# Turning the cached keys in 32x32 blocks on VectorE in place of 128x128 transposes on TensorE, in a decode kernel

## The chip, the cores and the metric

The kernel runs on one core of a Trainium2 chip; the other seven do nothing. The metric is the device time of one execution in microseconds, median of the runs. The core has TensorE (matrix multiplication, PE in the profile; PEld is its weight load), VectorE (DVE), ScalarE (ACT), GpSimd (POOL) and SyncE (SP), whose queue issues nearly all transfers here. All data is float32. [...]

## The reference, cut to what matters

One decode step of a transformer block for 8 sequences: a modulated layer norm, attention over a window of a cache, a projection, a second modulated norm and an MLP with squared ReLU.

```python
B, D, Hq, Hkv, Sk, Dh = 8, 512, 32, 8, 8192, 128     # W = 2048, rep = 4
mod = (silu(c) @ w_mod).reshape(8, 6, 1, -1)          # sa, ca, ga, sb, cb, gb
h = layernorm(x) * (1 + ca) + sa
q = (h @ wq)                                          # 8 x 32 heads x 128
k = repeat(k_cache[:, :, Sk - W:, :], rep, axis=1)    # last 2048 rows
v = repeat(v_cache[:, :, Sk - W:, :], rep, axis=1)
p = softmax(einsum("bhqd,bhkd->bhqk", q, k) * Dh ** -0.5)
o = einsum("bhqk,bhkd->bhqd", p, v)
x = x + ga * (o @ wo)
h = layernorm(x) * (1 + cb) + sb
x = x + gb * (relu(h @ w1 + b1) ** 2 @ w2 + b2)
```

K and V of the window are 67.1 MB each (8 x 8 x 2048 x 128 floats); with the weights about 165 MB come from HBM. Each key is used by four query heads only.

## The kernel before, in words

**Loads.** `pump` issues a list of loads in a fixed order on SP's queue. A load needs a free slot: there are two "big" slots (32 KB per partition, `K_SLOTS`) and five "small" ones (16 KB, `V_SLOTS`). A load whose slot isn't free makes SP wait, and all loads behind it wait too. `("K", q)` is a block of 4.2 MB: the keys of one KV head (`hk = q // 2`) for four sequences, on partitions `4 p + u` (`u` is the sequence, `p` runs over 32 pieces of the window), 64 cache rows of 128 floats each. `("V", v)` is 2.1 MB. The order is K0, four pieces of `w_mod`, four of `wq`, K1, V0, K2, V1, K3, V2, V3, K4, and from there on two V blocks to a K block, with three pieces of `wo` between them; at the end come the last part of `wo` with half of `w1` (`tail`, a big slot), the rest of `w1` (small) and `w2` (big). `done(key)` gives a slot back after the last instruction that reads it.

**Steps.** The attention runs in 32 steps `s` (half a K block each) and some more for the V blocks, which lag by `PV_LAG = 5` steps. In each step, for two of the four parts `g` of a K block:

- `transposes(q, g, e)` (L232, L234): TensorE turns eight 128x128 pieces, so that the head dimension lies on the partitions; the result is in PSUM (`kt_ps`). Two copies of 128x512, one by ACT and one by DVE, take it to `kT` in SBUF, sorted by sequence `u`. The last one of a block calls `done(("K", q))`.
- `scores(q, g)` (L358): four matmuls of 512 columns, one for each sequence `u`, side by side in four column groups of TensorE. They add into `s_ps`, whose rows are (u, part, query head); a window cut from `qwin` (queries between zeros) selects the rows.
- `weighted(v, h)` (L450): weights times V; then four DVE instructions (L464, L466) pick the diagonal blocks out of `o_ps`.

Once for each of the eight KV heads come `soft_a` to `soft_d` (copy of the scores, maximum, exponent at L402 on ACT, DVE copy at L410, eight TensorE transposes at L426 with two DVE multiplications at L429) and later `gather` and `project_o`.

**Order.** The program is written with a manual schedule: each engine executes its instructions in the order in which the code issues them. An instruction that waits holds back all behind it on its engine.

**Before the steps.** Modulation (L294), queries (L319), and `turn_q` (L330 to L334), which puts the queries on the partitions by head dimension (`qall`); `window` copies those of one KV head into `qwin` (L344). The first K block is turned early: `EARLY` lists its parts, three of which are turned between the matmuls of the modulation and the fourth in step 0.

Of the kernel before, what the change touches and what calls it, by code (L numbers as in the profile page):

```python
# [20 lines left out]
def tile_adaln_cached_attention_mlp(  # L21
# [34 lines left out]
    ktp = ctx.enter_context(tc.tile_pool(name="ktp", bufs=3))  # L56
    ps_kt = ctx.enter_context(tc.tile_pool(name="ps_kt", bufs=2, space=bass.MemoryType.PSUM))
# [127 lines left out]
    qall = consts.tile([P, HKV, B, REP], F32, name="qall")  # L185
    qwin = [consts.tile([P, B, 60], F32, name=f"qwin{i}") for i in range(2)]
    for t in qwin:
        nc.gpsimd.memset(t, 0.0)

# [8 lines left out]
    u4 = consts.tile([P, 4], F32, name="u4")  # L198
    nc.vector.tensor_reduce(u4, ident.rearrange("p (u x) -> p u x", u=4), axis=AX.X, op=ALU.add)
    for c in range(2):  # L200
        nc.vector.tensor_scalar(bq[:, 4 * c : 4 * c + 4], u4, uq[:, c : c + 1], None, op0=ALU.mult)
# [11 lines left out]

    mine = consts.tile([P, 2, REP], F32, name="mine")
    odd = ident.rearrange("p (r u) -> p u r", u=2)
    for u in range(2):
        nc.vector.tensor_reduce(mine[:, u, 0:1], odd[:, u, :], axis=AX.X, op=ALU.add)
        for t in range(1, REP):
            nc.vector.tensor_copy(mine[:, u, t : t + 1], mine[:, u, 0:1])

    KTS = {}

    def transposes(q, g, e):

        k = slot(("K", q), DH)
        if e == 0:
            KTS[q, g] = ktp.tile([P, 4, 16, 32], F32, name="kT")
        t = KTS[q, g]
        for a in range(2):
            p = ps_kt.tile([P, 4, P], F32, name="kt_ps")  # L230
            for i in range(4):
                nc.tensor.transpose(p[:, i, :], k[:, 32 * e + 16 * a + 4 * g + i, :], ident)  # L232
            i = 8 * e + 4 * a
            (nc.vector.tensor_copy if a else nc.scalar.copy)(  # L234
                t[:, :, i : i + 4, :], p.rearrange("p i (r u) -> p u i r", u=4)
            )
        if g == 3 and e == 1:
            done(("K", q))
# [24 lines left out]
    EARLY = [(0, g) for g in range(4)]  # L263
# [64 lines left out]
    def turn_q(r):  # L328
# [3 lines left out]
        for t in range(REP):  # L332
            nc.tensor.transpose(pT_[:, t * P : (t + 1) * P], qs[:, t * P : (t + 1) * P], ident)  # L333
        nc.vector.tensor_copy(  # L334
            qall[:, 4 * r : 4 * r + 4].rearrange("p g b t -> p t g b"),
            pT_.rearrange("p (t g b) -> p t g b", t=REP, g=4)[:, :, :, :B],
        )
# [4 lines left out]
    P_, PT_, RZ_, RZP_, OS_, O_, MX_, SS_ = {}, {}, {}, {}, {}, {}, {}, {}  # L342
    def window(hk):
        nc.vector.tensor_copy(qwin[hk % 2][:, :, 28:32], qall[:, hk])  # L344

    def scores(q, g):

        hk, c = divmod(q, 2)
        if c == 0 and g == 0:
            s_ps[0] = ps_1.tile([P, 512], F32, name="s_ps")  # L350
            if hk == 0:
                window(0)
        if c == 1 and g == 0 and hk + 1 < HKV:
            window(hk + 1)
        o = 28 - 4 * (2 * g + c)
        kT = KTS.pop((q, g))
        for u in range(4):
            nc.tensor.matmul(  # L358
                s_ps[0][32 * u : 32 * u + 32, :],
                qwin[hk % 2][:, 4 * c + u, o : o + 32],  # L360
                kT[:, u].rearrange("p i r -> p (i r)"),
                start=(c == 0 and g == 0),
                stop=(c == 1 and g == 3),
            )
# [8 lines left out]
    def soft_b(hk):  # L373
        pm = ps_m.tile([P, 512], F32, name="m_ps", tag="m_ps")
# [5 lines left out]
            pm[0:1, :P].rearrange("p (u g r) -> p u r g", u=4, g=4),  # L380
# [3 lines left out]
        nc.vector.tensor_scalar(  # L384
            mrow.rearrange("p u (g r) -> p u g r", g=4),
            m1.rearrange("p (u r) -> p u r", u=4)[:, :, None, :].to_broadcast([1, 4, 4, 8]),
            -SCALE,
            None,
            op0=ALU.mult,
        )  # L390
        MX_[hk] = mrow

    def soft_c(hk):
# [6 lines left out]
        pr = work.tile([P, 8, H, 2], F32, name="pr", bufs=1)  # L400
        z = work.tile([P, 1], F32, name="z")
        nc.scalar.activation(  # L402
            pr.rearrange("p i (r e) u -> p e i r u", e=2)[:, :, :, :, 0],
            SS_.pop(hk).rearrange("p (e i r) -> p e i r", e=2, i=8),
            AF.Exp,
            bias=nm,
            scale=SCALE,
            accum_out=z,
        )
        nc.vector.tensor_copy(pr[:, :, :, 1], pr[:, :, :, 0])  # L410
        zs = work.tile([P, B], F32, name="zs")
        nc.vector.tensor_scalar(zs, bq, z, None, op0=ALU.mult)  # L412
        P_[hk], RZP_[hk] = pr, zs
# [5 lines left out]
    def soft_d(hk):  # L419

        pr = P_.pop(hk)
        PT_[hk] = work.tile([P, 2, 4 * C, 4, 2 * REP], F32, name="pT", bufs=1)
        for a in range(2):
            pp = ps_m.tile([P, 512], F32, name="m_ps", tag="m_ps")
            for i in range(4):
                nc.tensor.transpose(  # L426
                    pp[:, i * P : (i + 1) * P], pr[:, 4 * a + i].rearrange("p r u -> p (r u)"), ident
                )
            nc.vector.tensor_mul(  # L429
                PT_[hk][:, a].rearrange("p x i r -> p i x r"),  # L430
                pp.rearrange("p (i x r) -> p i x r", i=4, r=2 * REP),
# [232 lines left out]
```

## Time and profile before

| | us |
|---|---|
| median of 3 runs | 397.13 (397.06 to 397.26) |
| the profiled execution: its time | 397.39 |
| the profiled execution: span, first to last instruction | 395.6 |
| PE busy | 330.5 (84%) |
| DVE busy | 178.2 (45%) |
| ACT busy | 97.5 (25%) |
| mean granted TensorE clock | 0.974 |

The page gives busy time for each engine and, in 40 slices, the share of the 16 DMA engines that was busy. A second view, of stretches of time, gives the same for windows that one chooses. The group rows read: line, engine, operation, result <- operands, shape, count | busy us in all, mean ns of one | idle time of the engine ahead of them and what ended it. The chain of waits goes back from the last instruction to what released each step; its rows are start, length, what. Waits of SP's queue (SPq) show when a load was held back for a slot.

### The profile page before, as it was taken

To read this page: it belongs to the slowest core of one execution; us is meant where nothing else is said; L and a number is where in the kernel's file an instruction comes from. 1 tells how busy PE (TensorE), PEld (TensorE's weight loads), DVE (VectorE), ACT (ScalarE), POOL (GpSimd) and SP (SyncE) were. 2 spreads that over 40 slices of the span, in tenths; PEclk is the share of its full clock that TensorE was granted. 3 is DMA by queue.
4 is the path that set the end of the run, shared out by engine and by line. 5 is a ranking of instruction groups with operands and counts; after the bars stand their busy time and mean duration, and the time that the engine had idled before them with its cause. 6 is when DMAs were issued, how large, how long until landed. Compare 5 with 4: busy or idle time off the path is not lost.

```text
span 395.6 us, 5981 instructions
## 1 busy us (share of the span) xinstructions
PE 330.5 (84%) x2550; PEld 162.4 (41%) x2550; DVE 178.2 (45%) x416; ACT 97.5 (25%) x169; POOL 2.4 (1%) x12
## 2 busy tenths in 40 slices
PE   0683489979998697999889988998859998997696
PEld 0440035554454353444444544444534454432133
DVE  6121023454456353655464556454524455455531
ACT  2220022342232122322332222222211241222010
POOL 2000000000000000000000000000000000000000
PEclk9996889999999998999999999999999999999999
DMA  8999999999999999999999999999999999999993
GB/s 335 410 430 427 441 418 442 417 419 446 404 435 442 414 432 422 441 417 451 403 449 409 444 416 434 434 419 421 437 419 447 417 437 413 431 431 421 422 424 136
DMA packets 10363, 165.22 MB, mean 418 GB/s; under 512 B 1112, under 2 KB 1376, under 8 KB 1632
## 3 DMA queue, kind: packets, MB, share of 16 engines
q1 hardware_dynamic: 10192, 164.71, 97.9%
q8 instruction: 20, 0.33, 0.3%
q10 hardware_dynamic: 144, 0.13, 0.1%
q14 instruction: 7, 0.06, 0.0%
HBM read 164.77 MB, written 0.07 MB: 417 GB/s over the span
## 4 chain that ended last, share of the span: by engine, by line
DMA 46%; PE 42%; DVE 7%; ACT 4%; issue 1%; ACTq 0%; DVEq 0%
DMA big<-in_A_k_cache_dram 31%; PE kt_ps L232 20%; PE s_ps L358 9%; PE o_ps L450 7%; DMA small<-in_A_wq_dram 6%; DMA big<-in_B_w_dram 5%; DMA small<-in_A_v_cache_dram 4%; ACT pr L402 2%; DVE o_sb L466 2%; DVE kT L234 2%; PE m_ps L294 1%; ACT kT L234 1%; DVE pT L429 1%; PE m_ps L319 1%; DVE pr L410 1%
## 5 line engine op out<-in xcount | busy, mean ns | idle before, releaser
L232 PE MATMUL kt_ps<-ident,big 128*128 128x128 f32 x1024 | 145.5, 285 | 22.6 <-DMA big<-in_A_k_cache_dram 18.3
L232 PEld LDWEIGHTS kt_ps<-ident,big 128*128 128x128 f32 x1024 | 112.8, 144 | 111.9 <-ACT kT L234 68.1
L234 DVE COPY kT<-kt_ps 128x512 f32<-128x512 f32 x128 | 88.2, 689 | 121.5 <-PE kt_ps L232 121.5
L234 ACT COPY kT<-kt_ps 128x512 f32<-128x512 f32 x128 | 75.0, 586 | 209.4 <-PE kt_ps L232 208.6
L358 PE MATMUL s_ps<-kT,qwin 128*32 128x512 f32 x512 | 69.2, 614 | 0.8 <-DVE qwin L344 0.8
L450 PE MATMUL o_ps<-small,pT 128*32 128x512 f32 x512 | 67.1, 602 | 1.9 <-DMA small<-in_A_v_cache_dram 1.9
L466 DVE SCALAR_TENSOR_TENSOR o_sb<-o_ps,diag,o_sb 128x128 f32<-128x128 f32 x96 | 33.7, 351 | 3.4
L319 PE MATMUL m_ps<-small,h1T 128*32 128x512 f32 x64 | 11.5, 857 | 11.5 <-DMA small<-in_A_wq_dram 11.5
L450 PEld LDWEIGHTS o_ps<-small,pT 128*32 128x32 f32 x512 | 11.7, 108 | 22.7 <-issue 22.7
L464 DVE TENSOR_SCALAR o_sb<-o_ps,diag 128x128 f32<-128x128 f32 x32 | 11.2, 350 | 16.3 <-PE o_ps L450 15.6
L358 PEld LDWEIGHTS s_ps<-kT,qwin 128*32 128x32 f32 x512 | 10.3, 109 | 12.8 <-issue 11.1
L402 ACT ACTIVATE pr<-ss,nm 128x512 f32<-128x512 f32 x8 | 9.9, 1244 | 11.8 <-DVE nm L399 11.7
L334 DVE COPY qall<-m_ps 128x128 f32<-128x128 f32 x2 | 0.8, 390 | 23.0 <-PE m_ps L333 23.0
L435 PE MATMUL m_ps<-zs,tsel 128*128 128x8 f32 x16 | 3.1, 266 | 8.7 <-DVE pT L429 8.7
L319 PEld LDWEIGHTS m_ps<-small,h1T 128*32 128x32 f32 x64 | 2.1, 134 | 19.8 <-DMA small<-in_A_wq_dram 10.6
L429 DVE TENSOR_TENSOR pT<-m_ps,mine 128x512 f32<-128x512 f32 x16 | 10.2, 680 | 0.0
L474 PE MATMUL m_ps<-o_sb,pick 128*128 128x512 f32 x16 | 8.4, 606 | 1.8 <-DVE o_sb L466 1.6
L426 PEld LDWEIGHTS m_ps<-ident,pr 128*128 128x128 f32 x64 | 6.9, 141 | 7.0 <-issue 7.0
L426 PE MATMUL m_ps<-ident,pr 128*128 128x128 f32 x64 | 8.7, 278 | 1.1 <-DVE zs L412 1.1
L370 DVE TENSOR_REDUCE mx<-ss 128x1 f32<-128x512 f32 x8 | 5.5, 688 | 8.6 <-ACT ss L368 8.6
L410 DVE COPY pr<-pr 128x512 f32<-128x512 f32 x8 | 3.4, 430 | 12.3 <-ACT pr L402 12.3
L294 PE MATMUL m_ps<-small,cT 128*32 128x512 f32 (+1 forms) x64 | 6.6, 531 | 1.3 <-DMA small<-in_w_mod_dram 1.3
(123 smaller groups left out, 105.4 us busy)
## 6 DMA issues: line engine op xcount, KB each, us to landing
big<-in_A_k_cache_dram SPq DMA_DIRECT2D x16, 4096.0 KB, 21.9
small<-in_A_v_cache_dram SPq DMA_DIRECT2D x32, 2048.0 KB, 23.2
small<-in_A_wq_dram SPq DMA_DIRECT2D x4, 2048.0 KB, 21.8
small<-in_w_mod_dram SPq DMA_DIRECT2D x4, 1536.0 KB, 17.4
small<-in_A_wo_dram SPq DMA_DIRECT2D x3, 2048.0 KB, 19.9
big<-in_A_wo_dram SPq DMA_DIRECT2D x2, 1024.0 KB, 17.8
big<-in_B_w_dram SPq DMA_DIRECT2D x1, 2048.0 KB, 23.4
big<-in_B_w_dram SPq DMA_DIRECT2D x1, 1792.0 KB, 22.0
```

The lines of the kernel that those rows point to most:

```text
L232: nc.tensor.transpose(p[:, i, :], k[:, 32 * e + 16 * a + 4 * g + i, :], ident)
L234: (nc.vector.tensor_copy if a else nc.scalar.copy)(t[:, :, i : i + 4, :], p.rearrange("p i (r u) -> p u i r", u=4))
L294: nc.tensor.matmul(pm[32 * q : 32 * q + 32, : (m1 - m0) * P].rearrange("p (m n) -> p m n", n=P), cT[:, kc, :], wv[:, m0:m1, q, :], start=( ...
L319: nc.tensor.matmul(pqs[r][32 * g : 32 * g + 32, :], hT[:, kc, :], w[:, 4 * r + g, :], start=(kc == 0), stop=(kc == NQ - 1),)
L358: nc.tensor.matmul(s_ps[0][32 * u : 32 * u + 32, :], qwin[hk % 2][:, 4 * c + u, o : o + 32], kT[:, u].rearrange("p i r -> p (i r)"), start ...
L402: nc.scalar.activation(pr.rearrange("p i (r e) u -> p e i r u", e=2)[:, :, :, :, 0], SS_.pop(hk).rearrange("p (e i r) -> p e i r", e=2, i= ...
L426: nc.tensor.transpose(pp[:, i * P : (i + 1) * P], pr[:, 4 * a + i].rearrange("p r u -> p (r u)"), ident)
L429: nc.vector.tensor_mul(PT_[hk][:, a].rearrange("p x i r -> p i x r"), pp.rearrange("p (i x r) -> p i x r", i=4, r=2 * REP), mine.rearrange ...
L450: nc.tensor.matmul(o[32 * g : 32 * g + 32].rearrange("p j d -> p (j d)"), PT_[hk][:, h, 4 * c + g].rearrange("p i r -> p (i r)"), v[:, j : ...
L464: nc.vector.tensor_scalar(d, o[:, 0, :], diag[:, 0:1], None, op0=ALU.mult)
L466: nc.vector.scalar_tensor_tensor(d, o[:, j, :], diag[:, j : j + 1], d, op0=ALU.mult, op1=ALU.add)
L474: nc.tensor.matmul(pp, pick.rearrange("p t u -> p (t u)"), o.rearrange("p c d -> p (c d)"), start=True, stop=True)
```

## The change

`transposes(q, j, e)` now is one DVE instruction, a transposition of 32x32 blocks: for 32 of the block's 64 cache rows it takes 32 of the 128 head dimensions (part `j`) and turns the 32 by 32 squares of each group of 32 partitions. A square's 32 columns are partitions `4 p + u`; they are written sorted by sequence, `u * 8 + p`, so that each sequence has runs of eight. In the order in which the engine writes, `u` runs fastest, with steps of eight floats. There is no `kt_ps` any more, and no copy of it.

Since a group of 32 partitions keeps its own pieces of the window, the result has on its partitions (group `i`, 32 dimensions) in place of 128 dimensions. The queries therefore are laid out as a block matrix over `i`: `turn_q` writes `qbd` with four copies on 32 partitions (L328), and `window` makes `qst` by one matmul with `sel` and eight small copies, four on ACT and four on DVE (L346). Row order of the scores changes; a matmul with a permutation (`perm`, L378) brings it back, and the exponent reads that result in PSUM and writes contiguously. The weights are turned by DVE too (L424, 1024 elements per partition), after two multiplications by a mask, one on DVE and one on ACT (L412, L410). `kT` has two buffers, not three; `EARLY` holds parts 0 and 1 of the first K block, where it held all four.

```diff
-    EARLY = [(0, g) for g in range(4)]
+    EARLY = [(0, 0), (0, 1)]
...
-        if kc < 3:
+        if kc < 2:
             transposes(0, kc, 0)
             transposes(0, kc, 1)
...
-    def transposes(q, g, e):
+    def transposes(q, j, e):
 
         k = slot(("K", q), DH)
         if e == 0:
-            KTS[q, g] = ktp.tile([P, 4, 16, 32], F32, name="kT")
-        t = KTS[q, g]
-        for a in range(2):
-            p = ps_kt.tile([P, 4, P], F32, name="kt_ps")
-            for i in range(4):
-                nc.tensor.transpose(p[:, i, :], k[:, 32 * e + 16 * a + 4 * g + i, :], ident)
-            i = 8 * e + 4 * a
-            (nc.vector.tensor_copy if a else nc.scalar.copy)(
-                t[:, :, i : i + 4, :], p.rearrange("p i (r u) -> p u i r", u=4)
-            )
-        if g == 3 and e == 1:
+            KTS[q, j] = ktp.tile([P, 64, 4, 8], F32, name="kT")
+        rows = slice(32 * e, 32 * e + 32)
+        nc.vector.transpose(
+            KTS[q, j][:, rows].rearrange("q r u p -> q r p u"),
+            k[:, rows, 32 * j : 32 * j + 32].rearrange("q r (p u) -> q r p u", u=4),
+        )
+        if j == 3 and e == 1:
             done(("K", q))
...
-        nc.vector.tensor_copy(
-            qall[:, 4 * r : 4 * r + 4].rearrange("p g b t -> p t g b"),
-            pT_.rearrange("p (t g b) -> p t g b", t=REP, g=4)[:, :, :, :B],
-        )
+        for j in range(4):
+            b = slice(32 * j, 32 * j + 32)
+            nc.vector.tensor_copy(
+                qbd[b, 4 * r : 4 * r + 4, j].rearrange("p g (b t) -> p t g b", t=REP),
+                pT_[b].rearrange("p (t g b) -> p t g b", t=REP, g=4)[:, :, :, :B],
+            )
...
     def window(hk):
-        nc.vector.tensor_copy(qwin[hk % 2][:, :, 28:32], qall[:, hk])
+
+        pq = ps_1.tile([P, 512], F32, name="q_ps")
+        nc.tensor.matmul(pq[:, :P], sel, qbd[:, hk].rearrange("p j x -> p (j x)"), start=True, stop=True)
+        pv = pq[:, :P].rearrange("p (j c u t) -> p c u j t", j=4, c=2, u=4)
+        for i in range(4):
+            b = slice(32 * i, 32 * i + 32)
+            for c in range(2):
+                (nc.vector.tensor_copy if c else nc.scalar.copy)(
+                    qst[hk % 2][b, 4 * c : 4 * c + 4, :, i, c], pv[b, c]
+                )
...
-                s_ps[0][32 * u : 32 * u + 32, :],
-                qwin[hk % 2][:, 4 * c + u, o : o + 32],
-                kT[:, u].rearrange("p i r -> p (i r)"),
+                s_ps[0][32 * u : 32 * u + 32, :].rearrange("q (r p) -> q r p", p=8),
+                qst[hk % 2][:, 4 * c + u, j].rearrange("p i c t -> p (i c t)"),
+                kT[:, :, u],
...
-        for a in range(2):
-            pp = ps_m.tile([P, 512], F32, name="m_ps", tag="m_ps")
-            for i in range(4):
-                nc.tensor.transpose(
-                    pp[:, i * P : (i + 1) * P], pr[:, 4 * a + i].rearrange("p r u -> p (r u)"), ident
-                )
-            nc.vector.tensor_mul(
-                PT_[hk][:, a].rearrange("p x i r -> p i x r"),
...
+        nc.vector.transpose(
+            PT_[hk].rearrange("p u j r -> p j u r"),
+            X_.pop(hk).rearrange("p j (u r) e c -> p j u (r e c)", u=4),
+        )
...
-        if s == 0:
-            transposes(0, 3, 0)
-            transposes(0, 3, 1)
```

Two places show how DVE's order moves. The first lies around the first scores. `qall` and `qbd` are the queries by head dimension, `qwin` and `qst` the queries as the score matmuls read them, `big_88` is the slot of K0 in the changed kernel and `big_89` that of K1. Before:

```order
L310 TENSOR_SCALAR mul<-m_ps,lo 128x128
L334 COPY qall<-m_ps 128x4x32
L344 COPY qwin_115<-qall 128x8x4
L234 COPY kT<-kt_ps 128x4x128 x2
L334 COPY qall<-m_ps 128x4x32
L234 COPY kT<-kt_ps 128x4x128 x3
L344 COPY qwin_116<-qall 128x8x4
L234 COPY kT<-kt_ps 128x4x128 x6
```

The same place in the changed kernel:

```order
L302 TENSOR_SCALAR mul<-m_ps,lo 128x128
L328 COPY qbd<-m_ps 32x4x4x8 x4
L346 COPY qst_112<-q_ps 32x16x4 x4
L328 COPY qbd<-m_ps 32x4x4x8 x4
L225 STREAM_TRANSPOSE kT<-big_88 128x32x8x4 x4
L225 STREAM_TRANSPOSE kT<-big_89 128x32x8x4 x3
L346 COPY qst_113<-q_ps 32x16x4 x4
L225 STREAM_TRANSPOSE kT<-big_89 128x32x8x4 x5
```

Before, the last copies of K0 (two on DVE) lie between the two `qall` copies. Now half of K0 (four transpositions) comes behind all copies of the queries, eight to `qbd` and four to `qst`, and K1 follows at once.

The second place is one softmax in the middle of the attention. Before:

```order
L370 TENSOR_REDUCE mx<-ss 128x1
L234 COPY kT<-kt_ps 128x4x128
L464 TENSOR_SCALAR o_sb<-o_ps,diag 128x128
L466 SCALAR_TENSOR_TENSOR o_sb<-o_ps,diag,o_sb 128x128 x3
L234 COPY kT<-kt_ps 128x4x128
L378 TENSOR_REDUCE m_1230<-m_ps 1x32
L384 TENSOR_SCALAR mrow<-m_1230 1x128
L234 COPY kT<-kt_ps 128x4x128
L399 COPY nm<-m_ps 128x1
L410 COPY pr<-pr 128x512
L412 TENSOR_SCALAR zs<-bq,z 128x8
L234 COPY kT<-kt_ps 128x4x128 x2
```

The same place in the changed kernel:

```order
L373 TENSOR_REDUCE mx<-ss 128x1
L225 STREAM_TRANSPOSE kT<-big_88 128x32x8x4
L458 TENSOR_SCALAR o_sb<-o_ps,diag 128x128
L460 SCALAR_TENSOR_TENSOR o_sb<-o_ps,diag,o_sb 128x128 x3
L225 STREAM_TRANSPOSE kT<-big_88 128x32x8x4
L384 TENSOR_REDUCE m_688<-m_ps 1x32
L390 TENSOR_SCALAR mrow<-m_688 1x128
L225 STREAM_TRANSPOSE kT<-big_88 128x32x8x4
L399 COPY nm<-m_ps 128x1
L412 TENSOR_SCALAR pr_704<-pr,uq 128x512
L414 TENSOR_SCALAR zs<-bq,z 128x8
L225 STREAM_TRANSPOSE kT<-big_88 128x32x8x4 x2
```

Each 128x512 copy of keys from PSUM has become a transposition of 1024 elements per partition, read straight from the slot; the number of DVE instructions for the keys stays the same, and ACT's copies of the same number are gone.

More of the change, by code (lines that the diff above doesn't have):

```diff
@@ L182, in tile_adaln_cached_attention_mlp @@
     s_ps = [None]
[L185 to L187 removed]
+    qbd = consts.tile([P, HKV, 4, B * REP], F32, name="qbd")
+    qst = [consts.tile([P, B, 4, 4, 2, REP], F32, name=f"qst{i}") for i in range(2)]
+    for t in [qbd, *qst]:
         nc.gpsimd.memset(t, 0.0)
```

74 lines of the change are left out of this document (31 added, 43 removed).

## The prediction

> **What bounds the kernel now.** I read the DMA part of the page first, then stretches of time, the chain of waits and the waits of SP's queue, last the groups by line and shape. The first fence has the page's DMA queue and the stretches (start:end, length, busy us and count by engine, granted clock, DMA share, GB/s).
>
> ```profile
> q1 hardware_dynamic: 10192, 164.71, 97.9%
> ```
>
> ```profile
> core 0: us, PE busy (x) PEld busy (x) DVE busy (x) ACT busy (x) POOL busy (x), PEclk, DMA share, GB/s
> 0.00:20.00 20.00, 7.69 (x42) 5.22 (x43) 8.64 (x42) 4.80 (x8) 2.43 (x12) 1.00 0.90 370
> 20.00:40.00 20.00, 12.08 (x96) 4.80 (x98) 4.31 (x9) 2.88 (x6) 0.00 (x0) 0.83 1.02 433
> 40.00:60.00 20.00, 12.93 (x90) 4.26 (x86) 2.34 (x5) 2.25 (x4) 0.00 (x0) 0.83 1.00 429
> 192.68:231.66 38.98, 36.18 (x280) 18.27 (x281) 20.45 (x44) 11.04 (x19) 0.00 (x0) 1.00 1.01 430
> ...
> 353.99:390.73 36.74, 28.57 (x237) 10.45 (x237) 17.20 (x52) 3.84 (x8) 0.00 (x0) 1.00 0.95 399
> 390.73:395.60 4.87, 1.72 (x48) 1.19 (x48) 0.58 (x2) 0.00 (x0) 0.00 (x0) 1.00 0.09 27
> ```
>
> The transfers bound it. From 20 us on the DMA engines are busy all the time at about 428 GB/s, although PE works 36.18 of 38.98 us in the stretch of four steps. The chain (start, length, what) and SP's longest wait show how close the two are:
>
> ```profile
> 211.35 20.18 DMA big<-in_A_k_cache_dram
> 231.66 1.07 PE kt_ps L232 x8
> ...
> 353.99 15.81 DMA small<-in_A_v_cache_dram
> 369.82 20.87 DMA big<-in_B_w_dram
> 390.73 1.76 PE m_ps L617 x48
> ```
>
> ```profile
> SPq L108 <- PE kt_ps L232: 250.9, 30, 27.3
> ```
>
> SP always waits until PE has turned a K block, then the next K takes 20.18 us to land, where 4.2 MB at 428 GB/s need 9.8: some 10 us of transfers are queued ahead of it. That reserve hides PE. Freeing PE therefore buys nothing while the transfers run without a gap; what can cost is a slot that comes free too late. Four steps need 39.0 us of transfers (two K, four V), 44 with a piece of `wo`.
>
> **The part that decides: one transposition.** Removed are 1024 PE transposes, 75.0 us of copies on ACT and 88.2 us on DVE; added are 128 DVE transpositions of 1024 elements per partition. The rows that bear on their price T:
>
> ```profile
> L232 PE MATMUL kt_ps<-ident,big 128*128 128x128 f32 x1024 | 145.5, 285 | 22.6 <-DMA big<-in_A_k_cache_dram 18.3 <-ACT kT L234 3.4
> ...
> L234 DVE COPY kT<-kt_ps 128x512 f32<-128x512 f32 x128 | 88.2, 689 | 121.5 <-PE kt_ps L232 121.5
> L234 ACT COPY kT<-kt_ps 128x512 f32<-128x512 f32 x128 | 75.0, 586 | 209.4 <-PE kt_ps L232 208.6 <-DVE kT L234 0.8
> ...
> L402 ACT ACTIVATE pr<-ss,nm 128x512 f32<-128x512 f32 x8 | 9.9, 1244 | 11.8 <-DVE nm L399 11.7
> ...
> L478 DVE STREAM_TRANSPOSE tr<-m_ps 128x512 f32<-128x512 f32 x8 | 5.7, 717 | 3.3 <-PE m_ps L474 3.3
> ...
> L334 DVE COPY qall<-m_ps 128x128 f32<-128x128 f32 x2 | 0.8, 390 | 23.0 <-PE m_ps L333 23.0
> L243 DVE STREAM_TRANSPOSE rc<-m_ps 128x448 f32<-128x448 f32 x1 | 0.7, 650 | 1.3 <-PE m_ps L598 1.3
> L554 DVE COPY at_i<-wo_ps 128x256 f32<-128x256 f32 x1 | 0.4, 425 | 1.2 <-PE wo_ps L490 1.2
> ...
> L276 ACT ACTIVATE sq<-xc_in,nmean 128x128 f32<-128x128 f32 x1 | 0.4, 402 | 5.9 <-DVE nmean L273 5.9
> ...
> L555 ACT COPY at_i<-wo_ps 128x256 f32<-128x256 f32 x1 | 0.4, 373 | 17.6 <-DVE at_i L554 17.6
> ```
>
> Lower end: both transpositions of before (717 and 650 ns) write contiguously. Their difference is 67 ns for 64 elements, 1.047 ns each, with 0.181 us fixed; T = 0.181 + 1024 x 1.047 = **1.25 us**.
>
> But the new ones write each float 32 bytes from the last (`u` fastest, steps of eight floats), and two instructions of before tell what single floats far apart cost. L334 writes floats 16 bytes apart: DVE copies of 512 and 256 elements (689, 425) give 1.031 ns an element and 161 ns fixed, so 128 should take 293 ns; it took 390, that is (390 - 161) / 128 = 1.79 ns an element. L402 on ACT also steps 16 bytes: ACT's rate is (586 - 373) / 256 = 0.832 ns, L276 is the same kind of instruction written contiguously, so 402 - 128 x 0.832 = 295 ns are fixed, and 1244 leaves (1244 - 295) / 512 = 1.85 ns. Two engines, different rates, nearly the same time per scattered float. I take 1.85, from the longer instruction: T = 0.181 + 1024 x 1.85 = **2.08 us** (2.01 by L334). Upper end: if the factor counts and not the time, ACT's 1.85 / 0.832 = 2.23 on DVE's 1.047 gives 2.33 ns, T = **2.57 us**.
>
> [...]
>
> **DVE's other work.** Besides the rows above:
>
> ```profile
> L466 DVE SCALAR_TENSOR_TENSOR o_sb<-o_ps,diag,o_sb 128x128 f32<-128x128 f32 x96 | 33.7, 351 | 3.4
> ...
> L464 DVE TENSOR_SCALAR o_sb<-o_ps,diag 128x128 f32<-128x128 f32 x32 | 11.2, 350 | 16.3 <-PE o_ps L450 15.6
> L429 DVE TENSOR_TENSOR pT<-m_ps,mine 128x512 f32<-128x512 f32 x16 | 10.2, 680 | 0.0
> ...
> L410 DVE COPY pr<-pr 128x512 f32<-128x512 f32 x8 | 3.4, 430 | 12.3 <-ACT pr L402 12.3
> ...
> L344 DVE COPY qwin<-qall 128x32 f32<-128x32 f32 x8 | 1.4, 173 | 0.1
> ```
>
> In the stretch of four steps DVE is busy 20.45 us, of which 16 key copies are 11.02; 9.43 remain. One softmax loses L410, two L429 and L344 (0.43 + 1.36 + 0.17 = 1.96). It gains a transposition of the weights, written in runs of eight floats (1.25 by the lower rate), a mask multiplication (0.68 like L429; up to 1.1 if its scattered reads cost 1.85 ns each), and four copies of 64 elements (0.21 each, L344's 173 ns and 32 more at 1.03): 10.23 us beside the keys. From K1 to K15 are 7.5 such pieces, 76.7 us; four of the 30 groups that follow V (L464 and three L466, 1.40 us) aren't due yet, nor half a softmax (4.6 / 2 = 2.3): 68.8 us. In each of seven softmaxes DVE also waits for the exponent: 12.3 / 8 = 1.54 us before, and 1.0 when ACT writes contiguously (295 + 512 x 0.832 = 721 ns in place of 1244): 7 us. Together 75.8 us.
>
> So four steps cost DVE 16 x 2.08 + 10.2 + 1.0 = 44.5 us against 39.0 of transfers. **DVE becomes the bound**, and the reserve of 10 us drains.
>
> **The start.** K0's second half now stands behind all query copies on DVE. Before:
>
> ```profile
> 53.60 0.38 DVE L334 COPY qall<-m_ps 128x128 f32<-128x128 f32 x1 [22.38 <-PE m_ps L333]
> ...
> 54.32 1.06 PE L358 MATMUL s_ps<-kT,qwin 128*32 128x512 f32 x8 [0.76 <-DVE qwin L344]
> ...
> 57.88 0.53 SPq L108 DMA_DIRECT2D big<-in_A_k_cache_dram  x1
> ...
> 58.52 0.66 PE L333 MATMUL m_ps<-ident,qs 128*128 128x128 f32 x4 [0.67 <-ACT qs L330]
> ```
>
> After: four `qbd` copies of that length (1.52 for 0.38), a matmul (about 0.4) and four small copies (0.83 for 0.17) move the first scores from 54.3 to 56.5; four of them take 0.53. ACT's second `qs` copy and the four transposes of the queries (0.66) end near 57.9, four more `qbd` copies near 59.6. Then come the four transpositions of K0, and K0's slot is free at 59.6 + 4T (before: K2's issue at 57.88); behind K2 in SP's queue stand V1 and K3. Loads up to V0 are 25.17 MB; by 60 us the three stretches have moved 20 x (370 + 433 + 429) = 24.64 MB, so V0 lands at 61.2. From issue to flow I take 1.8 us (the first 20 us lose (1 - 370 / 430) x 20 = 2.8, 0.7 of it before the first issue). With T = 2.08 K2 is issued at 67.9 and lands near 79.5; DVE, with K1 until 85, doesn't wait for it.
>
> **The end.** The last key copy of before, and what followed it:
>
> ```profile
> 351.18 0.69 DVE L234 COPY kT<-kt_ps 128x512 f32<-128x512 f32 x1 [0.91 <-PE kt_ps L232]
> ```
>
> It ended at 351.9, and the last V was issued 2.1 us later (353.99 in the chain), when its slot was free after the step's scores. From there 11.53 MB are left (V 2.10, `wo` 2.10, `w1` 3.67, `w2` 3.67), 26.9 us at 428 GB/s, and 4.9 us after the last landing (390.73 to 395.60). Before, 7 us of older transfers lay ahead; a queue that DVE has drained has none. So 2.1 + 1.8 + 26.9 + 4.9 = 35.7 us after the last transposition.
>
> **The sum.** 59.6 + 4T, then 120T + 75.8, then 35.7: span = 171.1 + 124 T = 428.8 with T = 2.08. The profiled execution's time lies 1.8 above its span (397.39 to 395.6), the median 0.3 below that: **430 us**.
>
> **At nothing.** PE loses 145.5 us, 18.2 of every four steps (145.5 / 8); of its 36.2 us there 18 remain, 22 at the clock of 0.83 that it had at 60% busy; score matmuls that read runs of eight may take twice their 0.53 without harm, since a `kT` buffer is needed again only two transpositions (4 us) later. ACT's multiplication and copies lie in the 75.0 us that it loses. Without that cover the doubled scores would add 1 us a softmax.
>
> **The rivals.**
> First, *scattered writes are free*: T = 1.25, four steps take DVE 31 us, and transfers stay the bound. K2 is issued at 59.6 + 5.0 = 64.6 and flows at 66.4: a gap of 5.2 us, never made up at a DMA share of 1.0. Span 400.8, **402 us**. For it: both transpositions seen ran at the full rate; against it: L334 and L402. This formula and the sum meet at T = 1.85. [...]
> Second, *the factor carries over* (T = 2.57): span 489.8, **491 us**. For it: 32 bytes is a longer step than any in the trace; against it: equal times on two engines.
> Third, on the other side, *no gap at all*: T = 1.25 and K2 issued by 61.2 - 1.8 = 59.4, from where the reserve holds. Then PE, ACT and DVE all have slack, and the 5% of idle DMA after 353.99 (1.8 us) may close: 397.1 to 395.3, or **396 us**. Against it: the order shows K0's last turns behind twelve copies that wait on each other.
>
> **How the numbers follow.** Forecast 0.55, its own range 412 to 455 (T from 1.93 to 2.28). First rival 0.24, second 0.12, third 0.06, 0.03 for prices in between. The range of 400 to 462 leaves out the third and nearly all of the second, about 2 in 10. This kernel's runs tell 0.2% from no change. Faster by more: 0.04, within: 0.05, both from the third and some of the rest; slower 0.91.
>
> **What would show it.** T is the mean of the transposition's group: near 2.08, DVE busy about 85 to 90% and the DMA share well under 1 from 60 us on, SP's waits on DVE, no wait of DVE for K. T near 1.25 proves me wrong on the write and leaves a gap of 5 us near 62 us alone. K2's issue near 68 and some 36 us from the last transposition to the end check the start and the end.

## The result, and the profile after

| | before | after |
|---|---|---|
| median of the runs beside each other, us | 397.19 (397.06 to 397.69, 4 runs) | 426.4 (423.18 to 428.78, 4 runs) |
| the profiled execution: time, span, us | 397.39, 395.6 | 428.78, 427.0 |

The ratio is 1.073, interval 1.065 to 1.080: the change makes the kernel 29 us slower, where 430 us and a range of 400 to 462 were forecast. The page of the changed kernel has these lines on the span, the engines and the DMA queue (busy us and share; then packets, MB, share):

```profile
span 427.0 us, 3775 instructions
...
PE 257.4 (60%) x1494; PEld 61.4 (14%) x1494; DVE 332.9 (78%) x430; ACT 33.5 (8%) x81; POOL 4.2 (1%) x13
...
q1 hardware_dynamic: 10192, 164.71, 91.9%
```

Before, transfers took 97.9% of 395.6 us, that is 387.3 us; now 91.9% of 427.0, 392.4. The same 164.71 MB move in nearly the same busy time, and the DMA engines stand still for 34.6 us where they stood still for 8.3. Stretches of time show where:

```profile
core 0: us, PE busy (x) PEld busy (x) DVE busy (x) ACT busy (x) POOL busy (x), PEclk, DMA share, GB/s
62.00:70.00 8.00, 2.69 (x16) 0.27 (x16) 7.97 (x7) 0.00 (x0) 0.00 (x0) 0.50 0.01 3
100.00:340.00 240.00, 147.49 (x812) 32.72 (x808) 217.93 (x252) 17.64 (x48) 0.00 (x0) 0.78 0.95 402
390.00:420.00 30.00, 25.91 (x165) 7.91 (x164) 16.33 (x49) 4.24 (x9) 0.00 (x0) 0.98 0.94 387
420.00:427.00 7.00, 3.84 (x114) 3.00 (x112) 0.58 (x2) 0.00 (x0) 0.00 (x0) 1.00 0.04 12
```

First a hole from 62 us on, in which almost nothing arrives (K2 is issued at 69.9, and its first packets start at 71.2; over 60 to 74 us the DMA share is 0.35, where it was 1.00 before, so some 9 us are lost); then a steady loss at 402 GB/s, against 427 before in the same stretch; at the end 387 GB/s and a tail without transfers. DVE is busy 7.97 us of the 8 in the hole and 217.93 of 240 in the middle. The groups by line, and the longest waits of SP's queue and of DVE (us in total, times, longest), name the owner:

```profile
L225 DVE STREAM_TRANSPOSE kT<-big 128x1024 f32<-128x1024 f32 x128 | 242.5, 1969 | 0.7 <-DMA big<-in_A_k_cache_dram 0.6
L346 DVE COPY qst<-q_ps 32x64 f32<-32x64 f32 x32 | 6.9, 216 | 7.4 <-ACT qst L346 7.4
L412 DVE TENSOR_SCALAR pr<-pr,uq 128x512 f32<-128x512 f32 x8 | 4.0, 498 | 8.6 <-ACT pr L402 8.6
```

```profile
SPq L107 <- DVE kT L225: 150.9, 9, 38.1
...
DVE m L384 <- PE m_ps L381: 9.2, 8, 2.8
DVE pr L412 <- ACT pr L402: 8.6, 8, 2.2
DVE qst L346 <- ACT qst L346: 7.4, 25, 0.9
DVE mx L373 <- ACT ss L371: 6.4, 6, 1.9
...
DVE o_sb L458 <- PE o_ps L444: 1.8, 4, 1.0
```

Before, SP's waits were mainly for PE's transposes, 250.9 us in all; now those for DVE's transpositions are the largest group, 150.9 us in all. DVE waits 0.6 us for a K block in the whole run: it sets the pace. One transposition takes 1.969 us from its start to its end; in a row they overlap a little, and the group's busy time divided by its count is 242.5 / 128 = 1.895 us each. That is the number that counts in a sum. The last rows of the chain of waits (start, length, what) show the end:

```profile
383.04 3.72 DVE kT L225 x2
386.81 1.06 PE s_ps L361 x8
...
397.15 7.28 PE o_ps L444 x64
404.46 0.36 DVE o_sb L458
...
420.65 3.24 PE m_ps L607 x112
```

From the last transposition (386.75) to the end of the span are 40.2 us, and in the chain all of them are compute: the last scores, the last softmax and weighted sum, projection and MLP follow one another with no wait for a transfer. Transfers ran beside them, though, at a share of 0.94 from 390 to 420 us (the third of the stretches above), and the last weights landed at about 420.1. Before, the chain ran through `small` and `big` loads in this place.

### The profile page after: what moved, and what is told of

Its sections match the earlier page's. It is cut to its first block, busy times and chain, and to the rows that moved or that the text cites. A ratio compares the mean times of both kernels' runs of the same rounds, so it can differ in the third digit from the quotient of the medians.

```text
span 427.0 us, 3775 instructions
## 1 busy us (share of the span) xinstructions
PE 257.4 (60%) x1494; PEld 61.4 (14%) x1494; DVE 332.9 (78%) x430; ACT 33.5 (8%) x81; POOL 4.2 (1%) x13
## 3 DMA queue, kind: packets, MB, share of 16 engines
q1 hardware_dynamic: 10192, 164.71, 91.9%
## 4 chain that ended last, share of the span: by engine, by line
DVE 52%; PE 18%; ACT 3%; issue 2%; ACTq 0%; DVEq 0%
DVE kT L225 38%; PE s_ps L361 7%; DVE o_sb L460 5%; PE o_ps L444 4%; PE p_ps L378 3%; DVE pT L424 2%; DVE o_sb L458 1%; ACT pr L402 1%; PE q_ps L541 1%; DVE qst L346 1%; DVE mx L373 1%; DVE tr L472 1%; ACT qst L346 1%; ACT ss L371 1%; DVE pr L412 1%
## 5 line engine op out<-in xcount | busy, mean ns | idle before, releaser
L225 DVE STREAM_TRANSPOSE kT<-big 128x1024 f32<-128x1024 f32 x128 | 242.5, 1969 | 0.7 <-DMA big<-in_A_k_cache_dram 0.6
L361 PE MATMUL s_ps<-kT,qst 128*32 128x512 f32 x512 | 96.9, 840 | 130.6 <-DVE kT L225 109.2
L444 PE MATMUL o_ps<-small,pT 128*32 128x512 f32 x512 | 83.3, 729 | 0.0
L361 PEld LDWEIGHTS s_ps<-kT,qst 128*32 128x32 f32 x512 | 11.8, 125 | 188.8 <-DVE kT L225 151.5
L444 PEld LDWEIGHTS o_ps<-small,pT 128*32 128x32 f32 x512 | 18.7, 128 | 49.5 <-issue 45.0
L328 DVE COPY qbd<-m_ps 32x128 f32<-32x128 f32 x8 | 3.0, 376 | 24.7 <-PE m_ps L325 24.7
L346 ACT COPY qst<-q_ps 32x64 f32<-32x64 f32 x32 | 6.5, 203 | 127.5 <-PE q_ps L341 94.4
L378 PE MATMUL p_ps<-ss,perm 128*128 128x512 f32 x16 | 15.9, 1098 | 0.0
L468 PE MATMUL m_ps<-o_sb,pick 128*128 128x512 f32 x16 | 13.5, 942 | 3.0 <-DVE o_sb L460 3.0
L346 DVE COPY qst<-q_ps 32x64 f32<-32x64 f32 x32 | 6.9, 216 | 7.4 <-ACT qst L346 7.4
L412 DVE TENSOR_SCALAR pr<-pr,uq 128x512 f32<-128x512 f32 x8 | 4.0, 498 | 8.6 <-ACT pr L402 8.6
L402 ACT ACTIVATE pr<-p_ps,nm 128x512 f32<-128x512 f32 x8 | 5.5, 687 | 60.1 <-DVE nm L399 60.1
L424 DVE STREAM_TRANSPOSE pT<-pr 128x1024 f32<-128x1024 f32 x8 | 9.8, 1230 | 0.0
L384 DVE TENSOR_REDUCE m<-m_ps 1x32 f32<-1x128 f32 x8 | 2.2, 278 | 9.2 <-PE m_ps L381 9.2
L410 ACT ACTIVATE pr<-pr,uq 128x512 f32<-128x512 f32 x8 | 6.8, 850 | 0.3
```

What stands on the lines that cost most here:

```text
L225: nc.vector.transpose(KTS[q, j][:, rows].rearrange("q r u p -> q r p u"), k[:, rows, 32 * j : 32 * j + 32].rearrange("q r (p u) -> q r p u ...
L346: (nc.vector.tensor_copy if c else nc.scalar.copy)(qst[hk % 2][b, 4 * c : 4 * c + 4, :, i, c], pv[b, c])
L361: nc.tensor.matmul(s_ps[0][32 * u : 32 * u + 32, :].rearrange("q (r p) -> q r p", p=8), qst[hk % 2][:, 4 * c + u, j].rearrange("p i c t -> ...
L378: nc.tensor.matmul(sp, perm, SS_.pop(hk), start=True, stop=True)
L424: nc.vector.transpose(PT_[hk].rearrange("p u j r -> p j u r"), X_.pop(hk).rearrange("p j (u r) e c -> p j u (r e c)", u=4),)
L444: nc.tensor.matmul(o[32 * g : 32 * g + 32].rearrange("p j d -> p (j d)"), PT_[hk][:, c, j : j + 4].rearrange("p i r -> p (i r)"), v[:, j : ...
```

## The experiments

The theory on trial: DVE is the bound because its transpositions write single floats far apart. The rivals in it are that something else in the instruction is slow (the transposition itself), that the low granted clock of TensorE is to blame, and that the hole at 62 us or the new order is.

### How the write's step sets the price

One kernel, in which the K blocks take turns in five patterns; the distance between successive floats in the write is 1, 2, 4, 8 or 16 floats. The sorting by sequence is left out, so the scores mix the sequences; the amount of work is the same. In each pattern the last index of the view runs fastest in the write.

```diff
-        nc.vector.transpose(
-            KTS[q, j][:, rows].rearrange("q r u p -> q r p u"),
-            k[:, rows, 32 * j : 32 * j + 32].rearrange("q r (p u) -> q r p u", u=4),
-        )
+        d = KTS[q, j][:, rows].rearrange("q r u p -> q r (u p)")
+        s = k[:, rows, 32 * j : 32 * j + 32]
+        w = q % 5
+        if w == 0:
+            nc.vector.transpose(d, s)
+        elif w == 1:
+            nc.vector.transpose(
+                d.rearrange("q r (p u) -> q r u p", u=2), s.rearrange("q r (u p) -> q r u p", u=2)
+            )
...
```

> The changed kernel with five write patterns, one for every fifth K block, each on its own line: successive floats of a transposition are written 1, 2, 4, 8 or 16 places... told as the distance of neighbours in the order of writing: 4 bytes (contiguous), 64, 32, 16 and 8 bytes. The sorting by sequence is left out (columns land in other places), so the scores are not those of the reference; the work is the same in size. [...] Rival (it is the read in rows of 128 bytes from the slot that is slow): all five near 1.97 us. Rival (only the distance of 32 bytes or more hurts): 16 bytes at 1.25.

The expectation names the same five distances in another order; the edit gives them in the order of its lines, 4, 8, 16, 32 and 64 bytes. The kernel ran once, in 403.75 us. The groups by line and shape, in that order:

```profile
L229 DVE STREAM_TRANSPOSE kT<-big 128x1024 f32<-128x1024 f32 x32 | 37.6, 1216 | 0.7 <-DMA big<-in_A_k_cache_dram 0.7
L231 DVE STREAM_TRANSPOSE kT<-big 128x1024 f32<-128x1024 f32 x24 | 28.2, 1216 | 0.0
L235 DVE STREAM_TRANSPOSE kT<-big 128x1024 f32<-128x1024 f32 x24 | 46.1, 1976 | 7.2 <-DMA big<-in_A_k_cache_dram 7.1
L239 DVE STREAM_TRANSPOSE kT<-big 128x1024 f32<-128x1024 f32 x24 | 45.9, 1975 | 1.3 <-DMA big<-in_A_k_cache_dram 1.3
L243 DVE STREAM_TRANSPOSE kT<-big 128x1024 f32<-128x1024 f32 x24 | 44.4, 1896 | 0.2 <-DMA big<-in_A_k_cache_dram 0.2
```

The price has one step, between 8 and 16 bytes: 1216 ns at 4 and 8, 1976 at 16, and no more at 32 or 64. All five read the slot in the same way, so the read isn't what is slow. The extra is (1976 - 1216) / 1024 = 0.74 ns a float. So the instruction is fast, the scattered write is slow, and from 16 to 64 bytes distance costs nothing further; the 32 bytes of the change cost no more than 16, the step of L334 and L402 that the prediction went by. The 1216 ns of the two upper rows lie near the 1.25 us worked out for the first rival. What in the hardware makes the step was not shown.

### The write made contiguous

`kT` keeps the sequence as its fastest index; the score matmul of a sequence then reads every fourth float.

```diff
-            KTS[q, j] = ktp.tile([P, 64, 4, 8], F32, name="kT")
+            KTS[q, j] = ktp.tile([P, 64, 8, 4], F32, name="kT")
...
-            KTS[q, j][:, rows].rearrange("q r u p -> q r p u"),
+            KTS[q, j][:, rows],
...
-                kT[:, :, u],
+                kT[:, :, :, u],
```

> The changed kernel with the sorting moved from the write to the read: the transposition writes contiguously, the score matmul reads every fourth float. The result is the same. Theory (scattered write makes DVE the bound): a transposition takes 1.25 us, DVE busy falls by about 128 x 0.7 = 90 us, the transfers are the bound again except for the gap at the start; K2's issue near 67, gap 7 to 8 us, time 403 to 406 us. Rival (what costs is the low TensorE clock and the hand-overs between the engines, not the write): 415 to 426 us, although a transposition takes 1.25. A slower read on TensorE (up to twice the 0.84 us) stays hidden by the theory.

Measured: 402.11 us (400.02 to 404.3, 10 runs), ratio 1.011 (1.008 to 1.014). The group of the transpositions, the DMA queue and a stretch in the hole:

```profile
L225 DVE STREAM_TRANSPOSE kT<-big 128x1024 f32<-128x1024 f32 x128 | 151.5, 1218 | 44.7 <-DMA big<-in_A_k_cache_dram 44.6
...
q1 hardware_dynamic: 10192, 164.71, 96.2%
...
64.00:66.00 2.00, 0.33 (x4) 0.20 (x8) 2.00 (x3) 0.00 (x0) 0.00 (x0) 0.93 0.00 0
100.00:340.00 240.00, 168.42 (x873) 33.54 (x872) 167.64 (x274) 18.20 (x48) 0.00 (x0) 0.89 1.01 429
```

With 0.71 us less for each transposition (1.895 to 151.5 / 128 = 1.184), DVE waits 44.6 us for K, transfers run at 429 GB/s again, and 24 of the 29 us are back; the time is a little under the 403 to 406 us expected. That is the cause, shown by undoing it alone. What remains is the hole: K2 is issued at 67.9 us, its first packets start at 69.2, and over 60 to 74 us the DMA share is 0.48, some 7 us lost. The profiled execution (404.3 us) is the slowest of the ten, so most of the others will have lost less. The time is that of the first rival, worked out as 402, but partly by luck: the rival counted K2's issue at 64.6 and a gap of 5.2 us.

The read has a price too. The trace has two rows for each of the four score matmuls of a group (512 rows for 256 matmuls), so "x8" is one group. One where the clock was full, of this kernel:

```profile
339.31 1.98 PE L361 MATMUL s_ps<-kT,qst 128*32 128x512 f32 x8 [0.84 <-DVE kT L225]
```

It took 1.06 us in the changed kernel (chain above, runs of eight floats). Reading every fourth float takes TensorE 1.9 times as long at full clock. At half the clock it takes hardly longer, 2.01 us (at 148.05 us, in a slice that the page gives 0.5), where the group with runs of eight takes 1.94 (at 302.98, granted 0.50): from half to full clock this read gains 0.03 us, that of runs of eight 0.88. What it costs the kernel is small, since PE has slack: the version sorted by pairs below, whose groups take 1.15 us, is 1.2 us faster in the median, and inside the spread of this one.

### The hole closed

The contiguous version, with the loads V1 and V2 ahead of K2 in the list, and the first piece of `wo` ahead of K4 (not in the cut below): loads whose slots are free while K0 is being turned.

```diff
-    loads = [..., ("K", 1), ("V", 0), ("K", 2)]
+    loads = [..., ("K", 1), ("V", 0), ("V", 1), ("V", 2), ("K", 2)]
```

> The kernel of the contiguous write (402.1 us) with another order of the loads: V1 and V2 ahead of K2, and the first piece of wo ahead of K4, so that SP's queue has transfers to issue while K0 is still being turned. Nothing else changes. Theory (its loss against the kernel before is the gap of some 8 us at the start, in which SP waits for K0's slot with nothing else to issue): the gap near 62 us is gone and the time falls by 6 to 8 us, to 394 to 396 us, under the kernel before. Rival (the loads taken ahead are missing later, K4 comes late instead): 398 to 401 us. Rival (the floor is the transfers of the kernel before): 397.

Measured: 398.33 us (397.56 to 398.86), ratio 1.0031 (1.0019 to 1.0042). The same stretch and the queue:

```profile
64.00:66.00 2.00, 1.73 (x12) 0.16 (x8) 2.00 (x3) 0.00 (x0) 0.00 (x0) 1.00 1.00 426
...
DMA  8999999999999999999999999999999999999993
...
q1 hardware_dynamic: 10192, 164.71, 97.8%
```

The hole is gone, and 3.8 us with it, but 394 to 396 was not reached; the median is 1.3 us above the 397.04 of the kernel before beside it. That is within the range of the rival that has loads come late (398 to 401) and above that of the floor (397). The row DMA (tenths of busy share in 40 equal slices of the span) has no second hole, and DVE waits 35.2 us for K in all, not the 44.6 of the version above, so late loads are not seen; but the profiled execution is the fastest of the six (397.56), and what the slower ones lose stays open. The DMA engines' busy time (share by span) is 97.8% of 395.8 = 387.1 us here, 96.2% of 402.5 = 387.2 with the hole, 387.3 before the change. These versions differ only in how long the engines stand still, and 8 to 9 us of that remain, most of it at the two ends. By an estimate from these numbers the transfers alone make 387 + 8 = 395 us of span; the kernel before, with 395.6, was there already.

Then also all copies to `qst` on ACT:

> The same with all copies to qst on ACT. Theory (transfers bound, DVE and TensorE have slack): within 1 us of the run with the new load order alone. Rival (DVE still sets part of the time): another 2 to 10 us less.

397.53 us (396.85 to 398.32, 11 runs), ratio 1.0008 (0.999 to 1.0026): not to be told from before. Copies that weigh 14 us where DVE is the bound (below) weigh less than 1 where the transfers are.

### The hole alone, in the kernel before

The kernel before with one piece of the change: only half of K0 is turned early, the rest behind the queries, as in the changed kernel, but by PE.

```diff
-    EARLY = [(0, g) for g in range(4)]
+    EARLY = [(0, 0), (0, 1)]
...
-        if kc < 3:
+        if kc < 2:
...
-        if s == 0:
-            transposes(0, 3, 0)
-            transposes(0, 3, 1)
```

> The kernel before with only half of K0 turned early, as the changed kernel has it: parts 2 and 3 are turned in step 1. TensorE still turns the keys. Theory (a K2 that is issued after V0 has landed opens a gap in the transfers that is never made up): K2 issued near 64 in place of 57.9, gap 4 to 5 us, time 400.5 to 402.5. Rival (the reserve of 10 us takes it up): 397 to 398.

399.2 us (398.71 to 399.4; before beside it 397.04), ratio 1.0053 (1.0039 to 1.0067): 2.2 us more, between the 400.5 to 402.5 of the theory and the 397 to 398 of its rival. K2 was issued at 61.89, not at the 64 that I had expected, and the share fell, lowest in this stretch:

```profile
64.00:66.00 2.00, 1.76 (x16) 1.27 (x12) 0.67 (x2) 0.58 (x1) 0.00 (x0) 1.00 0.64 279
```

By the prediction's rule (issue, 1.8 us to flow, V0's landing at 61.2) the hole is 61.9 + 1.8 - 61.2 = 2.5 us; over 60 to 74 us the share of 0.88 makes 1.7 us lost, and 2.2 came out at the end. So this hole wasn't made up later; that the theory's time was too long lies in my issue time.

### DVE relieved of copies

Of the changed kernel, only: all eight copies to `qst` on ACT.

```diff
-                (nc.vector.tensor_copy if c else nc.scalar.copy)(
+                nc.scalar.copy(
```

> The changed kernel with all eight copies to qst on ACT (before: four on DVE, four on ACT, which in the trace wait for each other, 1.95 us a head in place of 0.83). Theory (DVE sets the time, every us it loses counts): DVE loses 0.83 us of work and 1.1 us of waiting in each of seven heads, 13 us; time 411 to 416 us. Rival (TensorE's clock and the chain through it set the time): within 3 us of 426.

```profile
core 0: 411.7 us, clock 0.818
```

412.41 us (410.96 to 413.54), ratio 1.036 (1.030 to 1.041). DVE loses 6.9 us of busy time and 7.4 of waits for ACT, 14.3 together (the rows of L346 above), and the kernel falls by 14.0 in the medians (426.4 to 412.4). What DVE loses the kernel gains, about one to one: DVE sets the time. (For the same reason the gains of these experiments don't add up to 29 us: whatever relieves DVE counts, until the transfers are the bound again.) The granted clock stays at 0.82, so the gain isn't the clock's.

### Is it TensorE's clock?

The granted clock was 0.792 after the change, with PE busy 60% of the span, and 0.974 before, with 84%. Two kernels give TensorE additional matmuls (two of 512 columns, with unused results) to keep it busy. The first puts them behind each score group:

```diff
+        if q or j:
+            sp_ = ps_1.tile([P, 512], F32, name="q_ps")
+            for _ in range(2):
+                nc.tensor.matmul(sp_..., ident, ident..., start=True, stop=True)
```

> The changed kernel with two more 512-column matmuls on TensorE (results unused) behind each group of score matmuls, to keep TensorE busy and its clock up; nothing is taken away. Theory (DVE sets the time): granted clock over 0.9, time 418 to 428, the few us being DVE's waits for TensorE in the softmax (about 16 us in all, some of it clock). Rival (the low clock of 0.79 is what costs): 405 to 415 us.

It took 454.62 us (453.02 to 455.38), ratio 1.141 (1.135 to 1.148): neither account foresaw that. PE's groups and DVE's longest wait in it:

```profile
L371 PE MATMUL q_ps<-ident 128*128 128x512 f32 x252 | 137.1, 670 | 24.9 <-DVE qst L346 24.9
...
DVE o_sb L462 <- PE o_ps L448: 31.3, 19, 4.3
```

The clock rose to 0.93, but the added matmuls stood in PE's queue ahead of the weighted sums, for which DVE now waited 31.3 us (1.8 without them), and they themselves waited 24.9 us for copies out of the PSUM buffer that they share. PE, idle for a quarter of the span here (75% busy), was late all the same. As a test of the clock the run is spoilt.

The second puts the same two matmuls ahead of most score groups, where PE waits for a transposition anyway:

```diff
+        if q and not (c == 1 and j < 2):
+            sp_ = ps_1.tile([P, 512], F32, name="q_ps")
+            ...
         kT = KTS.pop((q, j))
```

> The changed kernel with two more 512-column matmuls (results unused) ahead of most groups of score matmuls, where TensorE waits for a transposition anyway, so that they don't stand in the way as in the run that had them behind. Theory (DVE sets the time; the low clock only lengthens DVE's waits for TensorE in the softmax, some 16 us in all): clock over 0.9, time 416 to 424. Rival (the low clock is the larger cost): under 412.

418.22 us (417.88 to 419.81), ratio 1.055 (1.053 to 1.056). The middle stretch and the span:

```profile
core 0: 416.1 us, clock 0.930
...
100.00:340.00 240.00, 187.45 (x975) 52.83 (x974) 223.49 (x258) 16.55 (x45) 0.00 (x0) 0.94 0.99 416
```

More work on PE made the kernel 8 us faster. DVE's wait for the maximum (9.2 us at L384) is down to 0.8, and the last transposition starts at 375.2 us (next fence, least, median and longest ns, first and last start), some 9.6 earlier than in the changed kernel:

```profile
L225 DVE STREAM_TRANSPOSE kT<-big x128: 1929/1972/2001, 13.4 to 375.2; 128x1024 f32<-128x1024 f32 x128
```

So about 8 of the 29 us go with these matmuls, about what that wait lost. The other 21 stay with PE at 0.93. That the clock acts through that wait is what the rows suggest; that nothing else in the added matmuls does was not tried apart.

### Sorted by pairs

In the ladder a step of 8 bytes cost no more than a contiguous write (1216 ns both). Here the write puts two neighbours side by side and then steps 64 bytes; the matmul reads every second float. The question is whether that costs either side.

```diff
-            KTS[q, j] = ktp.tile([P, 64, 4, 8], F32, name="kT")
+            KTS[q, j] = ktp.tile([P, 64, 2, 8, 2], F32, name="kT")
...
-            KTS[q, j][:, rows].rearrange("q r u p -> q r p u"),
-            k[:, rows, 32 * j : 32 * j + 32].rearrange("q r (p u) -> q r p u", u=4),
+            KTS[q, j][:, rows].rearrange("q r g p w -> q r p g w"),
+            k[:, rows, 32 * j : 32 * j + 32].rearrange("q r (p g w) -> q r p g w", g=2, w=2),
...
-                kT[:, :, u],
+                kT[:, :, u // 2, :, u % 2],
```

> The changed kernel with the keys sorted by pairs of sequences only: the write puts two neighbouring floats (8 bytes) side by side and then steps 64 bytes, the score matmul reads every second float. The result is the same. [...] Rival (reading every second float slows TensorE in proportion): eight matmuls at 1.3 to 1.5 us.

```profile
L225 DVE STREAM_TRANSPOSE kT<-big 128x1024 f32<-128x1024 f32 x128 | 151.6, 1219 | 44.5 <-DMA big<-in_A_k_cache_dram 44.4
...
340.19 1.15 PE L361 MATMUL s_ps<-kT,qst 128*32 128x512 f32 x8 [0.55 <-DVE kT L225]
```

400.9 us (400.78 to 400.95), ratio 1.008 (1.005 to 1.011). The write costs 1219 ns, as much as a contiguous one, and a group of score matmuls 1.15 us at full clock, between 1.06 for runs of eight and 1.98 for every fourth; the rival had 1.3 to 1.5. K2 is issued at 64.96 here, 3 us earlier than in the contiguous version's profile, and some 5 us of transfers are lost in the hole; the page gives 0.7 of the clock in the slice of 50 to 60 us here and 0.5 there, but that this makes the difference was not tried. With the load order and the ACT copies of above:

> The same with the other load order (V1 and V2 ahead of K2, wo ahead of K4) and with all copies to qst on ACT. Theory (the kernel before is at the floor of its transfers, about 387 us of DMA time and 8 us at both ends): 396.5 to 397.5, no measurable difference from the kernel before. Rival (TensorE's doubled read was holding something back): 394 to 396.

398.18 us (397.61 to 399.21, 12 runs; before beside it 397.24), ratio 1.0014 (0.9998 to 1.003). Again not to be told from the time of before, though its median lies 0.7 us above the 396.5 to 397.5 expected. Neither of the two best versions is below before, as the estimate of 395 us of span for the transfers would have it (spans 395.4 and 396.4 in their profiles).

## Why the prediction was right, term by term

**The bound** was named rightly: DVE replaces the transfers, and the write's step is the reason. The sum came out at 428.8 for the span, and 427.0 was measured, but four terms were off and cancelled (the predicted ones add up to 429.0 with T rounded):

| term | predicted | measured | difference |
|---|---|---|---|
| first transposition behind the queries | 59.6 | 62.45 | +2.9 |
| 124 transpositions | 257.9 (2.08 each) | 235.0 (1.895 each) | -22.9 |
| DVE's other work and waits up to the last | 75.8 | 89.3 | +13.5 |
| last transposition to the end | 35.7 | 40.2 | +4.6 |

That the number came so close is luck: one term was 22.9 us too long and three together 21.0 too short. With the measured T of 1.895 alone, the prediction's sum gives 171.1 + 124 x 1.895 = 406.1 us of span, or 407.6 as a time, which lies below its own range of 412 to 455. Its formula for the case that the transfers stay the bound gives 403.4 there (the two meet at T = 1.87, not at the 1.85 stated); the clear margin by which DVE was the bound came from the other three terms.

The measured numbers come from one stretch, from the first of the 124 to the end of the last, which the next fence shows as a whole and for L225 alone (324.30 - 235.02 = 89.3):

```profile
62.45:386.75 324.30, 193.59 (x1046) 41.61 (x1042) 293.66 (x324) 22.49 (x57) 0.00 (x0) 0.76 0.94 392
...
62.45:386.75 324.30, 235.02 (x124) 0.76 0.94 392
```

**T** was 5% to 10% too long: 1.969 us first to last, 1.895 in a row, against 2.08. It rested on 1.85 ns per scattered float, taken over from ACT's L402 with its 16-byte steps; with the same 0.181 us fixed, 1.969 us are 1.75 ns. The idea behind it held: the time per float carried over nearly from one engine to the other, the factor (second rival, 2.57) did not. The sum also lacked the overlap of successive transpositions.

**DVE's other work.** Its busy time was over-stated: 293.66 - 235.02 = 58.6 us, where 68.8 were counted. Its waits were under-stated: the step counted seven waits for the exponent (7 us; 7.8 in this stretch) and none of the others, but DVE stood idle 324.30 - 293.66 = 30.6 us. Most of the rest are three waits of the kind in the fence of waits above, 18.7 us in this stretch: for PE's maximum (8.4), for ACT's copy of the scores (4.6), and for ACT within the copies to `qst` (5.7). The last was visible in the code: the copies alternate between two engines, from one tile to one tile, and took turns, each waiting some 0.27 us for the other:

```profile
56.03 0.20 ACT L346 COPY qst<-q_ps 32x64 f32<-32x64 f32 x1 [4.31 <-PE q_ps L341]
56.27 0.21 DVE L346 COPY qst<-q_ps 32x64 f32<-32x64 f32 x1 [0.93 <-ACT qst L346]
56.51 0.20 ACT L346 COPY qst<-q_ps 32x64 f32<-32x64 f32 x1 [0.28 <-DVE qst L346]
...
57.73 0.23 DVE L346 COPY qst<-q_ps 32x64 f32<-32x64 f32 x1 [0.27 <-ACT qst L346]
...
57.84 1.93 PE L361 MATMUL s_ps<-kT,qst 128*32 128x512 f32 x8 [1.90 <-ACT qst L346]
59.70 0.72 PEld L325 LDWEIGHTS m_ps<-ident,qs 128*128 128x128 f32 x4 [1.66 <-issue]
59.70 1.12 PE L325 MATMUL m_ps<-ident,qs 128*128 128x128 f32 x4
```

**The start.** The same hand-overs explain part of it: 56.03 to 57.96 us for eight copies where 0.83 was counted. The first group of scores then took 1.93 us ahead of the second transposes of the queries, at a granted clock of 0.50; 0.53 was counted, which is half of the row "x8" of before, although that row is one group of four matmuls. The transposes took 1.12 for 0.66. K2's issue came at 69.9 (67.9 predicted), and the hole it makes was there as described; from issue to the first packets were 1.3 us, not 1.8 (and 2.8 less 0.7, from which 1.8 was taken, is 2.1).

**The end** was 4.6 us too short, and its reason was half right. The step let the remaining transfers set it: 30.8 us to the last landing, 4.9 after it. The transfers did run on, to about 420.1 us, 33.3 after the last transposition:

```profile
386.75:420.00 33.25, 29.11 (x181) 8.83 (x182) 17.59 (x51) 4.83 (x10) 0.00 (x0) 0.95 0.91 376
```

In the chain, though, there is only compute, which the step left out: the last softmax, the weighted sums of the last head (7.28 us for 64 rows of matmuls in a row) and the MLP up to the last 112 rows, which start at 420.65. Compute and transfers ended within about 0.6 us of each other; that either alone would have made nearly this time is an argument from that, not a run.

**At nothing.** Score matmuls in runs of eight cost no more than contiguous ones (1.06 us for a group, both kernels); PE's slack in time was real. But "hidden" was too simple in two ways: PE was granted 0.50 of its clock in the hole and 0.78 on the mean of the middle stretch, and 9.2 us of DVE's waits for PE went to 0.8 when added matmuls filled PE's waits (clock 0.930, 418.22 us); and it matters where in its queue an instruction stands (454.62 us).

**What would show it.** DVE was 78% busy, where 85 to 90% was said: T and the other work were shorter, the idle time longer. The rest came as said: SP waits for DVE, DVE doesn't wait for K.

**The rivals.** The first one's condition (T = 1.25) did not hold, but once the write was made contiguous its 402 us was measured as 402.11, with a shorter T and a later K2 than it had counted. The third's 396 was reached by no version: 397.53 at best.

## What to carry to other kernels

Before a layout change is moved into an instruction's access pattern, look for any instruction in the same trace that writes at that step, and take its time per element, not its ratio to another (here 1.85 ns, taken from L402, stood against a measured 1.75; the ratio gave 2.33). Writing two neighbouring floats side by side and reading every second one made the sorting free on DVE here (1219 ns, 1218 for the contiguous write) and nearly free on TensorE (1.15 us a group against 1.06). Where the transfers already run at a share of 1.0, work out their floor first: freeing an engine then gained nothing here (397.53 us at best, 397.04 before beside it), and a hole in the transfers stayed in the time.

## What was not expected of the hardware

- The price of a scattered write on DVE is a step: 1216 ns at 4 and 8 bytes, 1976 and 1975 at 16 and 32, and slightly less, 1896, at 64.
- TensorE's reading of its moving operand shows the like: at full clock a group of four score matmuls took 1.06 us from runs of eight floats, 1.15 from every second, 1.98 from every fourth. At half the clock the three took 1.94, 1.93 and 2.01: only the read of every fourth float hardly changed with the clock.
- TensorE was granted 0.50 while it waited for DVE at 62 to 70 us, and 0.78 on the mean of the middle stretch; with matmuls added in its waits 0.94, and the kernel was faster. Of four runs of the changed kernel the one with the highest clock was the fastest (423.18 us at 0.814) and the one with the lowest the slowest (428.78 at 0.792), but the two between are in the other order. The values between 0.50 and 1.00 are means: the clock record of the changed kernel's trace holds 25 stretches at 1.00, 25 at 0.50 and nothing else, that of the kernel before 5 of each.
